# Attention followed by a feed-forward layer: one dealt list of matmuls per slot, and the copied form of the softmax rows from head 14 instead of head 18

## The chip, the cores and the metric

The kernel runs on one core of one Trainium2 chip. The metric is the device time of one execution in microseconds (us). The median of several runs is compared.

## The reference

Eight batches of eight heads; each head has 576 tokens of width 64. Every head is causal attention with a decay bias, and the result of all heads goes through a normalised feed-forward layer with a residual. Cut to what matters:

```python
scores = q @ k.T / sqrt(64)                      # 576 x 576 for each of 64 heads
cum    = cumsum(log(clip(f, 1e-4, 1)))
scores = where(causal, -1e9, scores + cum[:, None] - cum[None, :])
attn   = exp(scores - max); attn = attn / (sum + 1e-9)
x      = concat over heads of attn @ v           # 8 x 576 x 512
xn     = (x - mean) / sqrt(var + 1e-6) * g
out    = x + relu(xn @ w1) @ w2                  # 512 -> 2048 -> 512
```

All is float32. The kernel gets it from float32r matmuls of a high and a low part (two or three matmuls for one product).

## The kernel before, in words

The instructions of every engine stand in the order in which the Python code emits them; no scheduler moves them. TensorE runs its list in that order, and each matmul has a weight load (the stationary operand) of its own.

The outer loop runs over **slots** `u`: head `n` has four slots, t = 1 to 4, for its query blocks of 64 + 128, 128, 128 and 128 rows. A slot is named (n, t) below, and u = 4n + t - 1. In one slot the code emits pieces of several heads at once, in an order given by a string of letters (`ORDERS`; the entry with the largest first slot not above `u` holds):

- `Q`: `qk_mm`, the score matmuls `s` of this slot (L374 high part with 128 rows, L375 low part and bias with 66 rows; tiles `hi`, `xq`, `kl`). `S`, `e`, `B`: the softmax of the rows on VectorE (L398), ScalarE (L409) and GpSimd (L416).
- `D`: `move`. For heads from `MOVED` on, the finished softmax rows `p` are copied by a DMA of the sync queue into a float32r tile `pq`.
- `t`: `transpose_unit`, TensorE transposes of the rows into `tr` (for (n, 1) three, (n, 2) three, (n, 3) four, (n, 4) five instructions). From `pq` they are float32r (L440), from `p` float32 (L442). A 64-column block gives an output of 64 rows, so its weights are 64 columns wide; the other blocks are 128 wide. `h`, `l`: ScalarE and VectorE take `tr` out as high part `ph` and low part `pl` (L492, L497).
- `A`: `av_unit`, attn times v into `o` (L527), after t = 2 and t = 4; `F`, `a`: its result goes to `xs` (L561, L572) and by DMA to memory.
- `M`, `r`, `m`, `N`, `R`: the feed-forward, one step per slot. A chunk is 256 tokens and has 16 steps. `M` (`mm1`) makes twelve matmuls `h` of 256 columns (L604 to L606) from the chunk's four split inputs `x`; `N` (`mm2`) makes six of 512 columns (L626 to L628) into `acc` for the step before, and after a chunk's last step `chunk_out` (L685 on VectorE, `xt`). `R` loads the next chunk: `xr` by DMA (two buffers), split into `x` on ScalarE (L588) and VectorE (L589). If the four `x` are not yet split when `M` comes (`moe.can`), the slot has no `h`. A chunk is loaded only when its tokens are finished: `moe.limit` is worked out from the slot and the lag.

The transposes of a slot come `lag` slots later: `LAG` = 2 for heads whose rows stay in `p`, `LAG_MOVED` = 4 for those that are copied; `A` one slot later still. So with four slots of lag, slot (n+1, 1) holds `o` of head n - 1 (t = 4), `tr` of (n, 1) and `s` of (n+1, 0) and (n+1, 1).

The feed-forward starts at slot 35 (`FIRST_MOE`). Its steps that are left after the last slot run one behind the other in a tail. Ahead of that, weights are decoded (`WPrep`, first part of the kernel). PSUM has a ring of six banks for `s`, `tr`, `o`, `h`, `xp` and two more for `acc`.

What the change touches: `MOVED` (L33) and the first slot of the third entry of `ORDERS` (L56), `qk_mm`, `tr`, `transpose_unit`, `av_unit`, and in the slot loop `piece`. `moe.limit` depends on `MOVED`.

Of the kernel before, what the change touches and what calls it, by code (L numbers as in the profile page):

```python
# [9 lines left out]
F32R = mybir.dt.float32r  # L10
# [19 lines left out]
W2_WAIT = 2  # L30
ALL = 2 * NCHUNK * FT + W2_WAIT
LAG, LAG_MOVED = 2, 4
MOVED = 18  # L33
FIRST_MOE = 35
WARM = 36

# [16 lines left out]
ORDERS = [  # L53
    (0, "WwbQsSthAeMrgFmlLNPaRf"),
    (37, "WwbQSstAMhPelgLNFrfmBRa"),
    (70, "WwAthQFlMSPNgreamLRDB"),  # L56
]


# [1 line left out]
def attn_moe(ctx: ExitStack, tc: tile.TileContext, qk, v, f, g, w1, w2, out):  # L61
    nc = tc.nc
# [9 lines left out]
    mm = nc.tensor.matmul  # L72

    def bank(name):
        return ps.tile([P, 512], F32, tag="b", bufs=6, name=name)
# [5 lines left out]
    identr = const.tile([P, P], F32R, tag="identr", name="identr")  # L81
# [3 lines left out]
    ident = identr.bitcast(F32)  # L85
# [221 lines left out]
    def load(n):  # L307
        h = Head()
        h.n, h.plain, h.full = n, n < NPLAIN, n < NFULL
        h.normal, h.moved = {}, {}  # L310
        h.lag = LAG if n < MOVED else LAG_MOVED
        if h.plain:
# [49 lines left out]

    def qk_mm(h, t):
        q0, m, w = QT[t]
        cuts = [(0, w)] if w <= 512 else [(0, w // 2), (w // 2, w)]
        h.s = getattr(h, "s", {})
        h.s[t] = []
        for i, (a, z) in enumerate(cuts):
            sp = bank(f"s{h.n}_{t}_{i}")[:m, : z - a]
            xq, kl = h.xq[:, q0 : q0 + m], h.kl[:, a:z]  # L370
            if h.plain:
                mm(sp, xq, kl, start=True, stop=True)  # L372
            else:
                mm(sp, h.hi[:, 0, q0 : q0 + m], h.hi[:, 1, a:z], start=True, stop=False)  # L374
                mm(sp, xq, kl, start=False, stop=True)  # L375
            h.s[t].append((a, z, sp))

    corners = []

# [54 lines left out]
    def rows_of(h, t):  # L434
        return h.moved.get(t, h.p[t][0])

    def tr(out_, in_):
        m = in_.shape[0]
        if in_.dtype == F32R:
            nc.tensor.transpose(out_.bitcast(F32R), in_, identr[:m, :m])  # L440
        else:
            nc.tensor.transpose(out_, in_, ident[:m, :m])  # L442

# [2 lines left out]
    def transpose_unit(h, t):  # L448
        n = f"{h.n}"
        pt = rows_of(h, t)  # L450
        work_ = []
        if t <= 2:
            if t == 1:
                h.ph1 = work.tile([P, 704], F32 if h.full else F32R, tag="ph1", bufs=1, name=f"ph1_{n}")
                h.pl1 = None if h.full else late.tile([P, 384], F32R, tag="pl1", bufs=1, name=f"pl1_{n}")
            ph = h.ph1
            pl = ph if h.full else h.pl1
            tp = bank(f"tr{n}_{t}")
            if t == 1:
                tr(tp[0:64, 0:128], rows_of(h, 0)[:, 0:D])  # L460
                tr(tp[0:64, 64:192], pt[:, 0:64])
                tr(tp[:, 192:320], pt[:, 64:192])
                work_.append((tp[0:64, 0:192], ph[0:64, 0:192], ph[64:128, 0:192]))
                work_.append((tp[:, 192:320], ph[:, 320:448], pl[:, 0:128]))
            else:
                tr(tp[0:64, 0:128], pt[:, 0:64])
                tr(tp[:, 128:256], pt[:, 64:192])
                tr(tp[:, 256:384], pt[:, 192:320])
                work_.append((tp[0:64, 0:128], ph[0:64, 192:320], ph[64:128, 192:320]))
                work_.append((tp[:, 128:384], ph[:, 448:704], pl[:, 128:384]))  # L470
        else:
            if t == 3:
                h.ph2 = work.tile([P, 9 * P], F32 if h.full else F32R, tag="ph2", bufs=1, name=f"ph2_{n}")
                h.pl2 = None if h.full else late.tile([P, 7 * P], F32R, tag="pl2", bufs=1, name=f"pl2_{n}")
            c = 0 if t == 3 else P
            ph = h.ph2[:, : 8 * P].rearrange("p (k c) -> p k c", k=4)[:, :, c : c + P]
            pl = None if h.full else h.pl2[:, : 6 * P].rearrange("p (k c) -> p k c", k=3)[:, :, c : c + P]
            tp = bank(f"tr{n}_{t}").rearrange("p (k c) -> p k c", k=4)
            tr(tp[0:64, 0, :], pt[:, 0:64])
            for k in range(1, 4):  # L480
                tr(tp[:, k, :], pt[:, 64 + P * (k - 1) : 64 + P * k])
            work_.append((tp[0:64, 0, :], ph[0:64, 0, :], ph[64:128, 0, :]))
            work_.append((tp[:, 1:4, :], ph[:, 1:4, :], pl))
            if t == 4:
                tp = bank(f"tr{n}_4b")[:, :P]
                tr(tp, pt[:, 64 + 3 * P : 64 + 4 * P])
                work_.append((tp, h.ph2[:, 8 * P :], None if h.full else h.pl2[:, 6 * P :]))
        h.parts = work_

    def transposed_hi(h, t):  # L490
        for tp, hi, lo in h.parts:
            nc.scalar.copy(out=hi, in_=tp)  # L492
# [5 lines left out]

    def av_unit(h, t):
        po = bank(f"o{h.n}_{t}")  # L500

        if h.full:
            def fac(o, k, mv, first=False):
                st, mv = (h.vr[0:64, 0], mv[0:64]) if k == 0 else (h.vr[:, k], mv)
                mm(o, st, mv, start=first, stop=True, skip_group_check=True)  # L505

            if t == 2:
                ph = h.ph1
                fac(po[0:64, 0:320], 0, ph[:, 0:320], True)
                fac(po[0:64, 64:320], 1, ph[:, 320:576])  # L510
                fac(po[0:64, 192:320], 2, ph[:, 576:704])
                h.o = (po, S1, 0)
            else:
                ph = h.ph2
                for k in range(4):
                    fac(po[0:64, 0:256], k, ph[:, 256 * k : 256 * k + 256], k == 0)
                fac(po[0:64, 128:256], 4, ph[:, 8 * P :])
                h.o = (po, S - S1, S1)
            return

        vv = h.vv

        def both(k):
            return vv[:, k].rearrange("p a d -> p (a d)")

        def acc(o, st, mv, first=False):
            mm(o, st, mv, start=first, stop=True, skip_group_check=True)  # L527

        if t == 2:
            ph, pl, w, c0 = h.ph1, h.pl1, S1, 0  # L530
            acc(po[:, 0:320], both(0), ph[:, 0:320], True)
            acc(po[:, 64:320], both(1), ph[:, 320:576])
            acc(po[:, 192:320], both(2), ph[:, 576:704])
            acc(po[0:64, 64:320], vv[:, 1, 0, :], pl[:, 0:256])
            acc(po[0:64, 192:320], vv[:, 2, 0, :], pl[:, 256:384])
        else:
            ph, pl, w, c0 = h.ph2, h.pl2, S - S1, S1
            for k in range(4):
                acc(po[:, 0:256], both(k), ph[:, 256 * k : 256 * k + 256], k == 0)
            acc(po[:, 128:256], both(4), ph[:, 8 * P :])  # L540
            for k in range(1, 4):
                acc(po[0:64, 0:256], vv[:, k, 0, :], pl[:, 256 * (k - 1) : 256 * k])
            acc(po[0:64, 128:256], vv[:, 4, 0, :], pl[:, 6 * P :])
        h.o = (po, w, c0)

    xs_tile = {}

# [225 lines left out]
    hd = {}  # L773
# [12 lines left out]
    for u, slot in enumerate(slots):  # L786

        def before(k):
            return slots[u - k] if u >= k else None

        if slot is not None:
            n, t = slot
            h = hd[n]
        def turn(more):

            for lag in (LAG, LAG_MOVED):
                b = before(lag + more)
                if b is not None and hd[b[0]].lag == lag:
                    return b
            return None  # L800

        av, av_t = None, 0
        if turn(1) is not None and turn(1)[1] in (2, 4):
            av, av_t = hd[turn(1)[0]], turn(1)[1]
        moe.fetch_low(ALL if wp.done() else wp.ready())
        want = moe.can(wp.ready()) and u >= FIRST_MOE

        def piece(c):
            tu = turn(0)
            if c == "t" and tu is not None:  # L810
                transpose_unit(hd[tu[0]], tu[1])
            elif c == "h" and tu is not None:
                transposed_hi(hd[tu[0]], tu[1])
            elif c == "l" and tu is not None:
                transposed_lo(hd[tu[0]])
            elif c == "Q" and slot is not None:
                if t == 1:
                    qk_mm(h, 0)
                qk_mm(h, t)
            elif c == "A" and av is not None:  # L820
                av_unit(av, av_t)
            elif c == "S" and slot is not None:
                if t == 1:
                    softmax_a(h, 0)
# [15 lines left out]
            elif c == "R":  # L840
                moe.limit = min(NCHUNK, max(0, u - (LAG if u < 4 * MOVED else LAG_MOVED) - 1) // (4 * H) * S // C)
                moe.rest()
# [6 lines left out]
            elif c == "D":  # L849
                if before(1) is not None and hd[before(1)[0]].n >= MOVED:  # L850
                    move(hd[before(1)[0]], before(1)[1])
# [38 lines left out]
        for c in [o for first, o in ORDERS if first <= u][-1]:  # L890
            piece(c)
# [48 lines left out]
```

## Time and profile before

| what | value |
|---|---|
| median of 3 runs | 1207.02 us (1204.66 to 1209.07) |
| profiled execution, its own time | 1205.75 us |
| its span (first to last instruction) | 1204.0 us |
| TensorE matmuls | 8140, busy 98% of the span |
| VectorE, ScalarE, GpSimd busy | 63%, 53%, 35% |
| sync DMA queue | 60.7% of 16 engines |

The engines: PE is TensorE's matmuls, PEld its weight loads (they run beside matmuls), DVE is VectorE, ACT ScalarE, POOL GpSimd, SP the sync engine with its DMA queue. In the rows of a timeline the columns are start, length, engine, line, operation, names (out<-in), shapes and count; successive instructions of one form are merged, and the length is then that of the group. A length of a matmul is from its start until it has drained, so successive matmuls overlap: what one costs the next is the distance of the starts. For a matmul "128*64 128x128" means weights of 128 rows and 64 columns, and 128 moving columns.

### The profile page before, as it was taken

Reading aid. Unit: us, or ns where it says so; the run is one execution under the profiler, and the core shown is the slowest. Engines: PE = TensorE matmul, PEld = TensorE weight load, DVE = VectorE, ACT = ScalarE, POOL = GpSimd, SP = SyncE. Lnnn points to the kernel's source line nnn. Section 1 sums busy time; section 2 is a strip of 40 time slices with the busy share of each in tenths; the row PEclk is TensorE's granted clock in tenths of the full one; section 3 lists DMA queues with packets and bytes.
Section 4 is the critical chain, followed back from the end, with each engine's and each line's share of the span. In section 5 each row is a group of like instructions: output and inputs, shape, how many; then the busy total and the mean of one; then the engine's idle time right before and its main releaser. Section 6 shows DMA issues by size and latency. Waiting matters only on the chain.

```text
span 1204.0 us, 25987 instructions
## 1 busy us (share of the span) xinstructions
PE 1185.4 (98%) x8140; PEld 1057.7 (88%) x8140; DVE 756.5 (63%) x2884; ACT 643.2 (53%) x1920; POOL 426.1 (35%) x533
## 2 busy tenths in 40 slices
PE   7998999999999999999999999999999999999998
PEld 5666889999999999989999999999999999999997
DVE  5787647676768676766767676767676764233232
ACT  5888655565656565556565555556565642112111
POOL 3568544343434434344434433434444320000000
PEclk8999999999999999999999999999999999999999
DMA  7788653557666767567676666657666654434433
GB/s 204 228 239 272 204 163 118 154 172 214 219 202 202 234 187 231 170 217 218 212 224 199 209 207 205 221 181 231 199 220 213 189 182 135 128 121 126 139 108 94
DMA packets 171481, 228.50 MB, mean 190 GB/s; under 512 B 40784, under 2 KB 107856, under 8 KB 171344
## 3 DMA queue, kind: packets, MB, share of 16 engines
q1 hardware_dynamic: 171344, 226.85, 60.7%
q8 instruction: 65, 1.06, 0.4%
q14 instruction: 72, 0.59, 0.1%
HBM read 157.46 MB, written 23.36 MB: 150 GB/s over the span
## 4 chain that ended last, share of the span: by engine, by line
PE 92%; DVE 3%; ACT 2%; DMA 2%; issue 1%; SPq 0%; POOL 0%; DVEq 0%; ACTq 0%; POOLq 0%
PE h L604 11%; PE h L605 11%; PE h L606 11%; PE acc L626 11%; PE acc L627 11%; PE acc L628 11%; PE o L527 6%; PE s L374 4%; PE tr L440 4%; PE s L375 3%; PE o L505 3%; PE tr L442 2%; PE s L372 2%; PE xp L649 1%; PE pc L191 1%
## 5 line engine op out<-in xcount | busy, mean ns | idle before, releaser
L416 POOL TENSOR_SCALAR p<-p,st 64x64 f32<-64x64 f32 (+4 forms) x320 | 172.5, 543 | 489.4 <-DVE st L415 196.7
L604 PE MATMUL h<-x,w1h 128*128 128x256 f32 x1152 | 330.0, 286 | 0.8 <-ACT xs L558 0.8
L605 PE MATMUL h<-x,w1h 128*128 128x256 f32 x1152 | 325.6, 283 | 1.4 <-DVE st L414 1.3
L606 PE MATMUL h<-x,w1l 128*128 128x256 f32 x1152 | 325.3, 282 | 0.0
L612 ACT ACTIVATE hh<-h 128x256 fp32r<-128x256 f32 x288 | 110.3, 383 | 303.3 <-PE h L606 303.0
L617 DVE SCALAR_TENSOR_TENSOR hh<-h,hh 128x256 fp32r<-128x256 f32 x288 | 121.1, 421 | 172.9 <-ACT hh L612 170.9
L626 PE MATMUL acc<-w2h,hh 128*128 128x512 f32 x576 | 226.6, 393 | 0.0
L627 PE MATMUL acc<-w2s,hh 128*128 128x512 f32 x576 | 226.4, 393 | 0.0
L628 PE MATMUL acc<-w2h,hh 128*128 128x512 f32 x576 | 225.1, 391 | 0.0
L604 PEld LDWEIGHTS h<-x,w1h 128*128 128x128 f32 x1152 | 218.8, 190 | 6.2 <-ACT xs L558 1.0
L605 PEld LDWEIGHTS h<-x,w1h 128*128 128x128 f32 x1152 | 219.2, 190 | 5.2 <-DVE x L589 2.0
L606 PEld LDWEIGHTS h<-x,w1l 128*128 128x128 f32 x1152 | 219.2, 190 | 0.0
L409 ACT ACTIVATE p<-p,st 64x64 f32<-64x64 f32 (+4 forms) x320 | 178.3, 558 | 49.2 <-DVE st L398 45.6
L492 ACT CAST ph<-tr 64x128 fp32r<-64x128 f32 (+4 forms) x416 | 117.8, 332 | 130.9 <-PE tr L440 76.5
L398 DVE CUSTOM_DVE_ANT_0 p<-s,mask 64x64 f32<-64x64 f32 (+4 forms) x320 | 130.7, 420 | 17.0 <-DMA pq<-p 5.2
L497 DVE TENSOR_TENSOR ph<-tr,ph 64x192 fp32r<-64x192 f32 x208 | 62.6, 301 | 108.7 <-ACT ph L492 83.6
L628 PEld LDWEIGHTS acc<-w2h,hh 128*128 128x128 f32 x576 | 108.2, 188 | 24.1
L626 PEld LDWEIGHTS acc<-w2h,hh 128*128 128x128 f32 x576 | 109.4, 190 | 12.6
L627 PEld LDWEIGHTS acc<-w2s,hh 128*128 128x128 f32 x576 | 109.3, 190 | 11.8
L374 PE MATMUL s<-hi 128*64 128x64 f32 x336 | 105.4, 336 | 1.3 <-POOL hi L352 1.0
L497 DVE TENSOR_TENSOR pl<-tr,ph 128x128 fp32r<-128x128 f32 x208 | 95.3, 458 | 4.6
L375 PE MATMUL s<-kl,xq 66*64 66x64 f32 x336 | 98.0, 296 | 0.0
(86 smaller groups left out, 1784.5 us busy)
## 6 DMA issues: line engine op xcount, KB each, us to landing
w2s<-w2d SPq DMA_DIRECT2D x288, 256.0 KB
raw<-in_qk_dram SPq DMA_DIRECT2D x56, 576.0 KB
wr<-in_w_dram SPq DMA_DIRECT2D x32, 512.0 KB
pq<-p SPq DMA_DIRECT2D x46, 288.0 KB
pq<-p SPq DMA_DIRECT2D x46, 224.0 KB
vr<-in_v_dram SPq DMA_DIRECT2D x64, 160.0 KB
out_dram<-xt SPq DMA_DIRECT2D x36, 256.0 KB
xq<-hi SPq DMA_DIRECT2D x56, 144.0 KB
```

The lines of the kernel that those rows point to most:

```text
L374: mm(sp, h.hi[:, 0, q0 : q0 + m], h.hi[:, 1, a:z], start=True, stop=False)
L375: mm(sp, xq, kl, start=False, stop=True)
L398: nc.vector.tensor_tensor_reduce(out=pt[:m, a:z], in0=sp, in1=mask[:m, off + a : off + z], scale=-SCALE, scalar=3.0e38 if i == 0 else st[: ...
L409: nc.scalar.activation(pt[:m, :w], pt[:m, :w], AF.Exp, bias=st[:m, i : i + 1], scale=-1.0, accum_out=st[:m, 2:3])
L416: nc.gpsimd.tensor_scalar(out=pt[:m, :w], in0=pt[:m, :w], scalar1=st[:m, 3:4], scalar2=1.0, op0=ALU.mult, op1=ALU.mult)
L497: nc.vector.tensor_tensor(out=lo, in0=tp, in1=hi.bitcast(F32), op=ALU.subtract)
L604: mm(ph, w1h[:, k, fs], c.x[k][:, 0, :], start=(k == 0), stop=False)
L605: mm(ph, w1h[:, k, fs], c.x[k][:, 1, :], start=False, stop=False)
L606: mm(ph, w1l[:, k, fs], c.x[k][:, 0, :], start=False, stop=(k == KT - 1))
L626: mm(c.acc[i], h[:, 0, ts_], w2h[:, j, :], start=(j == 0), stop=False)
L627: mm(c.acc[i], h[:, 0, ts_], low, start=False, stop=False)
L628: mm(c.acc[i], h[:, 1, ts_], w2h[:, j, :], start=False, stop=(j == FT - 1))
```

## The change

Two things. First, `MOVED` goes from 18 to 14 and the third order string starts at slot 56 instead of 70: heads 14 to 17 are copied and transposed in float32r, with four slots of lag. Second, the functions that made matmuls now return a list of them. For heads with a lag of four slots the piece `A` makes all three lists (`a` for attn times v, `b` for the transposes, `q` for the scores) and emits them in the order that `dealt` gives; in other heads the lists are emitted as before.

```diff
-MOVED = 18
+MOVED = 14
...
-    (70, "WwAthQFlMSPNgreamLRDB"),
+    (56, "WwAthQFlMSPNgreamLRDB"),
...
+    def dealt(t, u1, a, b, q):
+        if t == 4 and q:
+            return a[:5] + a[8:] + b[:2] + q[:1] + a[5:6] + b[2:] + q[1:2] + a[6:7] + q[2:3] + a[7:8] + q[3:]
+        if t == 4:
+            return a[:5] + a[8:] + b[:2] + a[5:6] + b[2:] + a[6:8]
+        if t == 2:
+            return a[:3] + a[4:] + b + a[3:4] + q
+        return (a + b if u1 else b[1:] + b[:1]) + q
...
+            if c in "AtQ" and tu is not None and hd[tu[0]].lag == LAG_MOVED:
+                if c == "A":
+                    a = av_unit(av, av_t) if av is not None else []
+                    b = transpose_unit(hd[tu[0]], tu[1])
+                    q = []
+                    if slot is not None:
+                        q = (qk_mm(h, 0) if t == 1 else []) + qk_mm(h, t)
+                    run(dealt(av_t, tu[1] == 1, a, b, q))
+            elif c == "t" and tu is not None:
+                run(transpose_unit(hd[tu[0]], tu[1]))
...
+                run((qk_mm(h, 0) if t == 1 else []) + qk_mm(h, t))
...
+                run(av_unit(av, av_t))
```

`a` for t = 4 has nine matmuls: four of 256 and one of 128 columns with weights 128 wide, then three of 256 and one of 128 with weights 64 wide.

**TensorE, slot (38, 1) before and now.** In the order of instructions `o36_4` is `a`, `tr37_1` is `b`, `s38_0` and `s38_1` are `q`; the last two numbers are the width of the weights and the moving columns. Before:

```order
L527 MATMUL o36_4_8690<-ph2_36_8572,vv36_8480 128x128
L527 MATMUL o36_4_8690<-pl2_36_8573,vv36_8480 64x256 x3
L527 MATMUL o36_4_8690<-pl2_36_8573,vv36_8480 64x128
L440 MATMUL tr37_1_8702<-identr_74,pq37_0_8557 64x128
L440 MATMUL tr37_1_8702<-identr_74,pq37_1_8559 64x128
L440 MATMUL tr37_1_8702<-identr_74,pq37_1_8559 128x128
L374 MATMUL s38_0_0_8708<-hi38_8474 64x64
L375 MATMUL s38_0_0_8708<-kl38_8475,xq8_1143 64x64
L374 MATMUL s38_1_0_8711<-hi38_8474 128x192
L375 MATMUL s38_1_0_8711<-kl38_8475,xq8_1143 128x192
```

The same slot of the change:

```order
L513 MATMUL o36_4_8730<-ph2_36_8607,vv36_8520 128x128
L513 MATMUL o36_4_8730<-pl2_36_8608,vv36_8520 64x128
L456 MATMUL tr37_1_8733<-identr_74,pq37_0_8597 64x128
L456 MATMUL tr37_1_8733<-identr_74,pq37_1_8599 64x128
L368 MATMUL s38_0_0_8734<-hi38_8514 64x64
L513 MATMUL o36_4_8730<-pl2_36_8608,vv36_8520 64x256
L456 MATMUL tr37_1_8733<-identr_74,pq37_1_8599 128x128
L368 MATMUL s38_0_0_8734<-kl38_8515,xq8_1143 64x64
L513 MATMUL o36_4_8730<-pl2_36_8608,vv36_8520 64x256
L368 MATMUL s38_1_0_8735<-hi38_8514 128x192
L513 MATMUL o36_4_8730<-pl2_36_8608,vv36_8520 64x256
L368 MATMUL s38_1_0_8735<-kl38_8515,xq8_1143 128x192
```

The three matmuls of 256 columns with narrow weights now stand between short matmuls and wide weights.

**TensorE, from slot (17, 3) to the first step of chunk 2.** `acc1` is the last `mm2` of chunk 1, `h2_0` the first `mm1` of chunk 2. Before:

```order
L628 MATMUL acc1_1_2612<-w2h_126,hh1_15_3490 128x512
L442 MATMUL tr17_2_3561<-identr_74,p17_2_3450 64x128
L442 MATMUL tr17_2_3561<-identr_74,p17_2_3450 128x128 x2
L374 MATMUL s17_4_0_3567<-hi17_3135 128x288
L375 MATMUL s17_4_0_3567<-kl17_3136,xq9_1286 128x288
L374 MATMUL s17_4_1_3570<-hi17_3135 128x288
L375 MATMUL s17_4_1_3570<-kl17_3136,xq9_1286 128x288
L604 MATMUL h2_0_3575<-x2_0_3435,w1h_124 128x256
```

The change, from the scores of the same slot (17, 4):

```order
L368 MATMUL s17_4_1_3554<-kl17_3125,xq9_1286 128x288
L513 MATMUL o16_4_3586<-ph2_16_3493,vv16_3402 128x256 x4
L513 MATMUL o16_4_3586<-ph2_16_3493,vv16_3402 128x128
L513 MATMUL o16_4_3586<-pl2_16_3494,vv16_3402 64x128
L456 MATMUL tr17_1_3589<-identr_74,pq17_0_3483 64x128
L456 MATMUL tr17_1_3589<-identr_74,pq17_1_3485 64x128
L368 MATMUL s18_0_0_3590<-hi18_3396 64x64
L513 MATMUL o16_4_3586<-pl2_16_3494,vv16_3402 64x256
L456 MATMUL tr17_1_3589<-identr_74,pq17_1_3485 128x128
```

Chunk 2 started in slot (17, 4); now slot (17, 4) has neither `h` nor `acc`, and `h2_0` comes behind `s18_1`. In the same way all later chunks up to chunk 5 start one slot later.

**VectorE, at the start of chunk 4.** `xt3` is `chunk_out` of chunk 3, `x4_2` and `x4_3` are splits for chunk 4, whose first step `h4_0` was in slot (26, 1) and is in slot (26, 2) now. Before, from the end of the softmax of (25, 4):

```order
L398 ISA st25_4_5595 128x1
L685 SCALAR_TENSOR_TENSOR xt3_0_5213<-acc3_0_4658,rs3_5216,xt3_0_5213 128x512
L685 SCALAR_TENSOR_TENSOR xt3_1_5344<-acc3_1_4659,rs3_5216,xt3_1_5344 128x512
L589 TENSOR_TENSOR x4_2_5609<-xr4_2_5562,x4_2_5609 128x256
L589 TENSOR_TENSOR x4_3_5612<-xr4_3_5565,x4_3_5612 128x256
L414 TENSOR_SCALAR st25_4_5595<-st25_4_5595 128x1
```

The change, one slot later:

```order
L404 ISA st26_1_5679 128x1
L358 CAST vv25_5687<-vr25_5479 128x5x64
L709 SCALAR_TENSOR_TENSOR xt3_0_5290<-acc3_0_4727,rs3_5293,xt3_0_5290 128x512
L709 SCALAR_TENSOR_TENSOR xt3_1_5435<-acc3_1_4728,rs3_5293,xt3_1_5435 128x512
L596 TENSOR_TENSOR xs24_320_5671<-o24_4_5647,ot24_320_5672 64x256
L613 TENSOR_TENSOR x4_3_5703<-xr4_3_5637,x4_3_5703 128x256
```

`x4_3` now waits behind `vv25`, `xt3` and `xs24`. In the kernel before, the same row of work (`vv33`, two `xt5`, `xs32`, `x6_3`) stands at the start of chunk 6, in slot (34, 1); there the change has the `xt5` behind `x6_3`, and slot (34, 1) has its `h`.

More of the change, by code (lines that the diff above doesn't have):

```diff
@@ L364, in qk_mm, with mm @@
         q0, m, w = QT[t]
+        todo = []
+        def mm(*a, **k):
+            todo.append(lambda: nc.tensor.matmul(*a, **k))
         cuts = [(0, w)] if w <= 512 else [(0, w // 2), (w // 2, w)]
@@ L376, in qk_mm @@
             h.s[t].append((a, z, sp))
+        return todo
     corners = []
@@ L435, in rows_of @@
         return h.moved.get(t, h.p[t][0])
[L437 to L442, printed above, removed]
     def transpose_unit(h, t):
@@ L450, in transpose_unit, with tr @@
         pt = rows_of(h, t)
-        work_ = []
+        work_, todo = [], []
+        def tr(out_, in_):
+            m = in_.shape[0]
+            if in_.dtype == F32R:
+                todo.append(lambda: nc.tensor.transpose(out_.bitcast(F32R), in_, identr[:m, :m]))
+            else:
+                todo.append(lambda: nc.tensor.transpose(out_, in_, ident[:m, :m]))
         if t <= 2:
@@ L488, in transpose_unit @@
         h.parts = work_
+        return todo
     def transposed_hi(h, t):
@@ L500, in av_unit, with mm @@
         po = bank(f"o{h.n}_{t}")
+        todo = []
+        def mm(*a, **k):
+            todo.append(lambda: nc.tensor.matmul(*a, **k))
         if h.full:
@@ L518, in av_unit @@
                 h.o = (po, S - S1, S1)
-            return
+            return todo
         vv = h.vv
@@ L544, in av_unit @@
         h.o = (po, w, c0)
+        return todo
+    def dealt(t, u1, a, b, q):
[6 more added lines that the diff above has]
+        return (a + b if u1 else b[1:] + b[:1]) + q
     xs_tile = {}
@@ L806, in attn_moe, with run @@
         want = moe.can(wp.ready()) and u >= FIRST_MOE
+        def run(todo):
+            for emit in todo:
+                emit()
         def piece(c):
             tu = turn(0)
-            if c == "t" and tu is not None:
-                transpose_unit(hd[tu[0]], tu[1])
+            if c in "AtQ" and tu is not None and hd[tu[0]].lag == LAG_MOVED:
[8 more added lines that the diff above has]
+                run(transpose_unit(hd[tu[0]], tu[1]))
             elif c == "h" and tu is not None:
@@ L816, in piece @@
             elif c == "Q" and slot is not None:
-                if t == 1:
-                    qk_mm(h, 0)
-                qk_mm(h, t)
+                run((qk_mm(h, 0) if t == 1 else []) + qk_mm(h, t))
             elif c == "A" and av is not None:
-                av_unit(av, av_t)
+                run(av_unit(av, av_t))
             elif c == "S" and slot is not None:
```

## The prediction

> **What bounds the kernel now.** I read the page first: engines, the slices, the chain.
>
> ```profile
> span 1204.0 us, 25987 instructions
> PE 1185.4 (98%) x8140; PEld 1057.7 (88%) x8140; DVE 756.5 (63%) x2884; ACT 643.2 (53%) x1920; POOL 426.1 (35%) x533
> PEclk8999999999999999999999999999999999999999
> PE 92%; DVE 3%; ACT 2%; DMA 2%; issue 1%; SPq 0%; POOL 0%; DVEq 0%; ACTq 0%; POOLq 0%
> ```
>
> TensorE is the bound, at full clock nearly everywhere. So a gain must come from shorter TensorE work, and "busy" does not say whether a step is stream or weight load. For that I took the timeline of matmuls, and of weight loads, in slot (46, 1), whose list is the first one shown with the change.
>
> ```profile
> 701.51 0.70 PE L527 MATMUL o<-ph,vv 128*128 128x256 f32 x5
> 702.05 0.58 PE L527 MATMUL o<-pl,vv 128*64 128x256 f32 x4
> ```
>
> The next two are two steps of `h` in slot (46, 2).
>
> ```profile
> 706.46 0.28 PE L604 MATMUL h<-x,w1h 128*128 128x256 f32 x1
> 706.58 0.28 PE L605 MATMUL h<-x,w1h 128*128 128x256 f32 x1
> ```
>
> The starts of two matmuls of 256 columns are 0.12 us apart. The first group is four of 256 and one of 128: 0.54 - 0.48 = 0.06 for 128 columns. So a stream costs some 0.03, 0.06, 0.09, 0.12 for 64, 128, 192, 256 columns (the first and third are estimates in proportion).
>
> ```profile
> 702.62 0.13 PEld L374 LDWEIGHTS s<-hi 128*64 128x64 f32 x1
> 702.68 0.14 PEld L375 LDWEIGHTS s<-kl,xq 66*64 66x64 f32 x1
> 702.74 0.19 PEld L374 LDWEIGHTS s<-hi 128*128 128x128 f32 x1
> 702.85 0.19 PEld L375 LDWEIGHTS s<-kl,xq 66*128 66x128 f32 x1
> 702.96 0.19 PEld L604 LDWEIGHTS h<-x,w1h 128*128 128x128 f32 x1
> ```
>
> The other slot shows loads for wide transposes:
>
> ```profile
> 705.88 0.23 PEld L440 LDWEIGHTS tr<-identr,pq 128*128 128x128 f32 x2
> 706.05 0.19 PEld L374 LDWEIGHTS s<-hi 128*128 128x128 f32 x1
> ```
>
> In the first of these fences the loads set the pace: 0.055 to 0.06 apart where they are 64 wide, 0.11 where 128 wide, though the streams beside them are only 0.03 to 0.09. Loads for float32r transposes, 128 wide, are 0.17 / 2 = 0.085 apart. The rule that I take from this: a step lasts as long as the longer of its own stream and the load of the next matmul. Long matmuls (256, 512 columns) hide every load; short ones ahead of wide weights do not.
>
> By the Trainium skill (TensorE: Matmul & The Clock Gate, section LDWEIGHTS) a load takes columns / 1.2 ns, 53 and 107 ns, whatever the rows. The ordinary loads agree, 66 rows included; the transposes' 85 do not. With 107 for them the dealing would give 0.07 us more a head, 3.3 in all; I go by 85.
>
> **The change, part by part.** *Dealing, by slots of a head.* Only the part of a load that sticks out counts. For (n, 1), before: narrow transpose to wide 0.025, `s` 64 to 64 0.025, 64 to 192 0.08, 192 to 192 0.02, 192 to `h` 0.02; sum 0.17. Now: two narrow scores ahead of a narrow `o` 0.025 each, the last one ahead of `h` 0.02; sum 0.07. Saved 0.10. For (n, 3): three steps into wide transposes 0.025 each and one into the scores 0.05; now a 256-column matmul stands ahead of the scores; saved 0.05. For (n, 2) and (n, 4): the narrow transpose goes last, so the first wide load lies under a 512-column matmul; saved 0.025 each. Together 0.20 a head (0.21 with prices to the ns), for 50 heads 10.6 us. Six of the new neighbours of a head (a score ahead of `o`, a wide transpose ahead of a score and the like) stand in no row; such a step can cost from its stream alone to 0.05 more, the excess of a load of 0.11 over a stream of 0.06. I take the rule's value, since the narrow rows 702.62 to 702.74 are the nearest, and give the range 0.01 for each, 3 us in all.
>
> *Float32r in heads 14 to 17.* Fifteen transposes a head change form.
>
> ```profile
> 249.74 0.60 PE L442 MATMUL tr<-identr,p 128*64 128x128 f32 x4
> 250.18 0.27 PE L442 MATMUL tr_4b<-identr,p 128*128 128x128 f32 x1
> 250.21 0.36 PE L604 MATMUL h<-x,w1h 128*128 128x256 f32 x1
> 250.41 0.28 PE L605 MATMUL h<-x,w1h 128*128 128x256 f32 x1
> ```
>
> From the first transpose to the second `h` it is 0.67; less 0.12 for the first `h`, 0.55 for five, 0.11 each, 1.64 a head. In copied form, in the old order, by the rule: 0.06 + 0.085 + 0.06 in (n, 1); 2 x 0.085, 3 x 0.085 and 4 x 0.085, each with 0.11 for the load of the scores, in the others; 1.30. Saved 0.35, for four heads 1.4. Sum with the dealing 12.0; all instructions of both orders priced one by one give 12.1, which I take.
>
> *Copies.* Twenty more DMAs on the sync queue. One issue:
>
> ```profile
> 703.77 0.47 SPq L431 DMA_DIRECT2D pq<-p  x1
> ```
>
> That is 20 x 0.47 = 9 us of queue time in 16 slots, over some 62 us; behind them stand `w2s`, `xr` and `raw`, all fetched a slot or more ahead. I price them at nothing, with up to 1 us of waiting if that cover is gone. GpSimd does the same work.
>
> *Later ends.* In (n, 1) the last matmul of `o` ends 0.37 later (1.31 instead of 0.94 after 701.51, so 702.8), and the first scores start 0.5 earlier, in a bank that `tr_4b` held.
>
> ```profile
> 699.86 0.28 DVE L497 TENSOR_TENSOR pl<-tr_4b,ph 128x128 fp32r<-128x128 f32 x1
> 703.41 0.37 ACT L561 COPY ot<-o 64x256 f32<-64x256 f32 x1
> ```
>
> ScalarE takes `o` only at 703.41, and the bank was free by 700.14; both are covered by more than 0.5 us. Price nothing; without that cover it would be up to 0.4 us in two slots of each head, 40 us, which I count with the slower side.
>
> *Chunk starts.* The slots without `h` move. What they cost now, with a like slot beneath each:
>
> ```profile
> 241.52:245.35 3.83, 3.83 (x29) 3.51 (x29) 2.72 (x9) 1.52 (x4) 0.43 (x1) 1.00 0.15 44
> 256.46:260.50 4.04, 3.60 (x30) 3.22 (x29) 3.80 (x12) 1.89 (x6) 1.83 (x3) 1.00 0.82 274
> 384.81:387.72 2.91, 2.52 (x22) 2.12 (x19) 2.83 (x11) 2.86 (x9) 0.68 (x1) 1.00 0.83 294
> 400.07:403.39 3.32, 3.32 (x27) 2.99 (x25) 2.55 (x12) 2.66 (x9) 1.36 (x2) 1.00 0.60 205
> 512.72:528.44 15.72, 13.99 (x87) 11.96 (x86) 10.56 (x40) 7.70 (x24) 6.23 (x8) 0.89 0.75 231
> 531.77:544.08 12.31, 12.31 (x93) 11.44 (x92) 7.04 (x26) 6.16 (x18) 4.97 (x7) 1.00 0.67 214
> ...
> 700.59 0.39 PE L628 MATMUL acc<-w2h,hh 128*128 128x512 f32 x1
> 700.82 0.39 PE L626 MATMUL acc<-w2h,hh 128*128 128x512 f32 x1
> ```
>
> (Columns: stretch, length, busy time and count of PE, PEld, DVE, ACT, POOL, clock, DMA share, GB/s.) Six `mm2` matmuls are 6 x 0.23 = 1.38, missing in the first slot of a late chunk. Slot (26, 1) lost 2.91 - (3.32 - 1.38) = 1.0; slots (34, 2) to (34, 4) lost 15.72 - (12.31 - 1.38) = 4.8; slot (17, 4), against (16, 4) less `mm2`, with five `o` more (0.50) and four float32 transposes for three (0.11),, lost 4.04 - 3.06 = 1.0. Sum 6.8. My prices give 12.26 for the undisturbed three slots, so the rule holds to half a per cent.
>
> ```profile
> 251.72 0.40 PE L626 MATMUL acc<-w2h,hh 128*128 128x512 f32 x1
> 253.54 0.42 DVE L617 SCALAR_TENSOR_TENSOR hh<-h,hh 128x256 fp32r<-128x256 f32 x1
> 258.26 0.41 DVE L589 TENSOR_TENSOR x<-xr,x 128x256 fp32r<-128x256 f32 x1
> ...
> 513.91 1.39 DVE L685 SCALAR_TENSOR_TENSOR xt<-acc,rs,xt 128x512 f32<-128x512 f32 x2
> 514.57 0.39 PE L604 MATMUL h<-x,w1h 128*128 128x256 f32 x1
> 515.56 0.41 DVE L589 TENSOR_TENSOR x<-xr,x 128x256 fp32r<-128x256 f32 x1
> 516.02 0.38 PE L605 MATMUL h<-x,w1h 128*128 128x256 f32 x1 [1.06 <-DVE st L414]
> ```
>
> At chunk 6 TensorE stood from 514.57 to 516.02 for the last split `x`, which VectorE did behind `xt`; after it the granted clock fell (0.89 in that stretch). After the change: chunk 6 has its `h` in (34, 1) and `x` ahead of `xt`, so 0 (0 to 1). Chunk 4 gets VectorE's order of the old chunk 6, so 4.8 (1 to 5, the low end being what it loses today). Chunk 2 has two slots without `h`: from `hh` of the last step to the last `x` VectorE took 258.26 - 253.54 = 4.7; now the list between has also the `tr16_4` parts, two more splits and the softmax of (17, 4), less `vv`, some 2.7 more. From the end of that `h` TensorE has two `mm2` (2.8), three `o` and `tr` groups with their scores (3.6) and nine `h` (1.2), 7.6 us, until it needs the last `x`; `hh` starts 1.8 after that end (251.72 to 253.54), so VectorE is ready at 1.8 + 7.4 + 0.4 = 9.6; a wait of 2, with the clock after it 3.5 (1.3 to 6). Sum 8.3 against 6.8: 1.5 lost.
>
> *Sum.* 12.1 - 1.5 = 10.6. The profiled execution took 1205.75, of it 1204.0 span and 1.75 around it: 1195.2. The median of the runs is 1.27 above it, 1207.02: **1196.4 us**.
>
> **The rivals.**
>
> *Switching widths empties the array (slower).* Changes between weights 64 and 128 wide go from 10 to 14 a head, 200 in all. Price, from the row
>
> ```profile
> L605 PE MATMUL h<-x,w1h 128*128 128x256 f32 x1152 | 325.6, 283 | 1.4 <-DVE st L414 1.3
> ```
>
> 0.283 - 0.12 = 0.16 of fill and drain that is now hidden: 32 us, so 1228. It turns the result from 10.6 / 200 = 0.053 us a switch. Against it: in the first fence the group ends with a wide matmul of 128 columns ahead of a narrow one and that step took 0.06, its stream. The Trainium skill (TensorEngine Tiling (Array Packing), section Key Properties) says that changing the tiling mode drains TensorE; the switches of this trace show no such drain. Chance 0.04.
>
> *Heavy chunk starts.* All three at their upper ends, 12 instead of 8.3: 1200.1, with a move's wait of 1, 1201. For it: the DMA share of 0.75 to 0.83 there; against: VectorE's list is lighter at chunk 6. Chance 0.13. *Light chunk starts*, 2.3 in all: 1190.4. Chance 0.12.
>
> *The dealing does nothing*, if the 0.11 belongs to the score matmuls and not to what stands ahead of their loads: only 1.4 - 1.5, so 1207. Against it: `s` to `h` costs the same 0.11, and a load beside 512 columns none. Chance 0.05.
>
> **How the numbers follow.** The forecast keeps 0.66; its own range is 1193 to 1200 (stalls 2.5 either way, 1 to 3 for the prices). With heavy and half of the light starts, and runs that lay 2 us about their median, 1191 to 1202. A measurement tells 0.3%, 3.6 us, from no change. Faster: forecast, heavy, light, 0.91; within: dealing does nothing, 0.05; slower: the drain, with the lost cover of the later ends, 0.04.
>
> **What the new profile would show.** Weight loads 0.11 apart gone between the scores of (n, 1); a quiet head some 0.21 us shorter; heads 14 to 17 without L442-like float32 transposes; waits for `x` near (18, 1) and (26, 2), none near (34, 2). I am wrong if the quiet heads keep their length, if TensorE waits for `pq` or `o` in each slot, or if the clock falls at more than two chunk starts.

## The result and the profile after

The changed kernel took 1198.99 us in the median (1198.44 to 1199.87, 4 runs), the kernel before 1207.29 on the same chip (1204.66 to 1209.07, 4 runs). The ratio is 0.9934, 95% interval 0.9914 to 0.9953: 8.3 us faster, 6 to 10 by the interval. Forecast were 10.6 us and 1196.4.

The page of the changed kernel: span, busy times, clock by slices, shares of the chain of waits.

```profile
span 1198.1 us, 26129 instructions
PE 1178.0 (98%) x8140; PEld 1051.9 (88%) x8140; DVE 756.9 (63%) x2884; ACT 644.2 (54%) x1920; POOL 427.1 (36%) x533
PEclk8998999999999999999999999999999999999999
PE 93%; DMA 2%; DVE 2%; ACT 2%; issue 1%; POOL 0%; SPq 0%; DVEq 0%; ACTq 0%; POOLq 0%
```

TensorE is still the bound, with as many instructions; 7.4 us of its busy time and 5.8 of the weight loads' are gone. The two profiled spans differ by 5.9 us. Slot (13, 1), ahead of the first changed slot, already starts 1.0 us later in this profile (181.43 against 180.39 us). That is not the change. The 8 in the fourth slice of PEclk is a stretch from 106.0 to 112.8 us, ahead of the first changed slot, in which the granted clock was 0.50; the kernel before has none there. Of the profiles that are alike up to slot (13, 1), those with this stretch have the slot at 181.4 to 182.1 (the changed kernel, e1, e7), those without it at 179.3 to 180.5 (before, e2, e3). Behind the slot the gain is 6.9.

The next two fences are from the timelines of matmuls, before and after. Each holds the first `o` of a slot (n, 1) and the same of the next head. Between them lies one quiet head, one without the extra matmuls of a chunk's end.

```profile
638.19 0.70 PE L527 MATMUL o<-ph,vv 128*128 128x256 f32 x5
653.83 0.70 PE L527 MATMUL o<-ph,vv 128*128 128x256 f32 x5
```

```profile
510.17 0.70 PE L513 MATMUL o<-ph,vv 128*128 128x256 f32 x5
525.67 0.70 PE L513 MATMUL o<-ph,vv 128*128 128x256 f32 x5
```

15.64 us before, 15.50 now: 0.14 saved a head, where 0.21 was forecast. This is the main miss, and it repeats: from head 36 to head 63 the two profiles part by 3.8 us, 0.14 a head.

To see where it is lost I split every slot into its list (from the first matmul of the list to the first `h`) and the rest (twelve `h`, six `acc`). Medians over the quiet slots behind 560 us, in us:

| slot | list before | list after | rest before | rest after | saved | priced |
|---|---|---|---|---|---|---|
| (n, 1) | 1.535 | 1.441 | 2.834 | 2.835 | 0.093 | 0.107 |
| (n, 2) | 0.580 | 0.547 | 2.817 | 2.818 | 0.033 | 0.028 |
| (n, 3) | 1.272 | 1.243 | 2.804 | 2.846 | -0.013 | 0.053 |
| (n, 4) | 0.991 | 0.954 | 2.807 | 2.817 | 0.027 | 0.028 |

Three slots came out as priced, to 0.014 us. Slot (n, 3) gained nothing.

The weight loads of slot (n, 1) in the new kernel, behind those of the five wide `o`:

```profile
604.46 0.17 PEld L456 LDWEIGHTS tr<-identr,pq 128*64 128x64 f32 x2
604.57 0.13 PEld L368 LDWEIGHTS s<-hi 128*64 128x64 f32 x1
604.63 0.14 PEld L513 LDWEIGHTS o<-pl,vv 128*64 128x64 f32 x1
604.71 0.14 PEld L456 LDWEIGHTS tr<-identr,pq 128*128 128x128 f32 x1
604.80 0.14 PEld L368 LDWEIGHTS s<-kl,xq 66*64 66x64 f32 x1
604.87 0.14 PEld L513 LDWEIGHTS o<-pl,vv 128*64 128x64 f32 x1
604.93 0.19 PEld L368 LDWEIGHTS s<-hi 128*128 128x128 f32 x1
```

The run of loads 0.11 apart between short scores is gone: wide loads now alternate with narrow ones, under a narrow `o` of 256 columns, at spacings of 0.06 to 0.09.

The slot that gained nothing. First from the timeline of before, a slot (n, 3): the four transposes in one row, the two scores, the first `h`, then the first `acc` and the first row of the next list.

```profile
583.14 0.45 PE L440 MATMUL tr<-identr,pq 128*64 128x128 f32 x4
583.43 0.44 PE L374 MATMUL s<-hi 128*128 128x448 f32 x1
583.70 0.37 PE L375 MATMUL s<-kl,xq 66*128 66x448 f32 x1
583.91 0.28 PE L604 MATMUL h<-x,w1h 128*128 128x256 f32 x1
...
585.34 0.40 PE L626 MATMUL acc<-w2h,hh 128*128 128x512 f32 x1
...
586.72 0.29 PE L440 MATMUL tr<-identr,pq 128*64 128x128 f32 x2
```

The same of the new kernel, in slot (30, 3), and then the `acc` of slot (31, 3), one head later:

```profile
455.50 0.47 PE L456 MATMUL tr<-identr,pq 128*64 128x128 f32 x4
455.81 0.30 PE L513 MATMUL o<-pl,vv 128*64 128x256 f32 x1
455.95 0.37 PE L368 MATMUL s<-hi 128*128 128x448 f32 x1
456.15 0.37 PE L368 MATMUL s<-kl,xq 66*128 66x448 f32 x1
...
457.80 0.40 PE L650 MATMUL acc<-w2h,hh 128*128 128x512 f32 x1
...
459.18 0.28 PE L456 MATMUL tr<-identr,pq 128*128 128x128 f32 x2
...
473.26 0.40 PE L650 MATMUL acc<-w2h,hh 128*128 128x512 f32 x1
...
474.67 0.38 PE L456 MATMUL tr<-identr,pq 128*128 128x128 f32 x3
```

Two things show. In the list, from the first transpose to the second score it took 0.56 before (583.14 to 583.70) and 0.65 now, with one more matmul of 256 columns (0.12) in it: 0.03 saved, where the step counted 0.05. And the six `acc`, which nothing in the change touches, take 1.38 us at 455 but 1.41 at 473, by the same instructions in the same order and at full clock. From head 31 on slot (n, 3) is in that slower rhythm in all heads but one; heads 20 and 22 to 24 had it too, heads 27 to 30 did not. The kernel before already had it in one head of four: where the list of (n, 3) begins with four transposes for a chunk's end (`xp`), its six `acc` take 1.40 us. More on it below.

Chunk 2. The fences show stretches of the new kernel (columns as in the prediction; each runs from the first scores with 128-wide weights of one slot to those of the next, so it holds the next slot's `o` and `tr`), then matmuls with the waits in front of them, then VectorE.

```profile
254.29:258.80 4.51, 2.25 (x20) 1.87 (x19) 4.27 (x14) 2.16 (x7) 0.67 (x2) 1.00 0.77 242
258.80:262.21 3.41, 2.62 (x20) 2.10 (x19) 2.05 (x11) 3.00 (x9) 0.67 (x1) 1.00 0.85 236
```

```profile
257.31 0.78 PE L513 MATMUL o<-ph,vv 128*128 128x256 f32 x5 [2.25 <-DVE ph L506]
...
260.38 0.38 PE L628 MATMUL h<-x,w1h 128*128 128x256 f32 x1 [0.39 <-ACT x L612]
...
254.21 1.41 DVE L709 SCALAR_TENSOR_TENSOR xt<-acc,rs,xt 128x512 f32<-128x512 f32 x2
255.53 0.47 DVE L596 TENSOR_TENSOR xs<-o,ot 64x320 f32<-64x320 f32 x1
255.93 0.74 DVE L613 TENSOR_TENSOR x<-xr,x 128x256 fp32r<-128x256 f32 x2
...
256.97 0.28 DVE L506 TENSOR_TENSOR ph<-tr,ph 64x128 fp32r<-64x128 f32 x1
```

By the prediction's prices the two slots last 2.86 and 1.42 us too long, 4.3 in all (3.5 forecast). The long wait is not for `x`: TensorE stood 2.25 us for `ph`, which VectorE reached only behind `xt`, `xs` and two splits. The wait for `x` came later and was short.

Chunk 4, the same views:

```profile
386.07:390.96 4.89, 3.47 (x27) 2.82 (x25) 4.76 (x19) 3.03 (x11) 2.78 (x5) 1.00 0.84 205
390.96:396.51 5.55, 3.80 (x27) 3.18 (x26) 1.60 (x6) 1.81 (x6) 2.61 (x3) 1.00 0.86 304
```

```profile
389.13 0.38 PE L629 MATMUL h<-x,w1h 128*128 128x256 f32 x1 [0.99 <-DVE st L420]
...
396.08 0.45 PE L456 MATMUL tr<-identr,pq 128*128 128x128 f32 x3 [1.75 <-DMA pq<-p]
```

Losses of 2.34, 1.90 and 0.49 in (26, 2) to (26, 4), 4.7 together (4.8 forecast). The first holds the wait of 0.99 for the last split `x` (VectorE's split at 388.66 ended at 389.07) and one of 0.41 for `ph` behind it. The second is the copy `pq`, which the forecast priced at nothing. Chunk 6 has no wait: its slot (34, 2) starts and goes through at the pace of a quiet one.

### The profile page after: what moved, and what is told of

Its sections match the earlier page's. It is cut to its first block, busy times and chain, and to the rows that moved or that the text cites. A ratio compares the mean times of both kernels' runs of the same rounds, so it can differ in the third digit from the quotient of the medians.

```text
span 1198.1 us, 26129 instructions
## 1 busy us (share of the span) xinstructions
PE 1178.0 (98%) x8140; PEld 1051.9 (88%) x8140; DVE 756.9 (63%) x2884; ACT 644.2 (54%) x1920; POOL 427.1 (36%) x533
## 3 DMA queue, kind: packets, MB, share of 16 engines
q8 instruction: 65, 1.06, 0.4%
## 4 chain that ended last, share of the span: by engine, by line
PE 93%; DMA 2%; DVE 2%; ACT 2%; issue 1%; POOL 0%; SPq 0%; DVEq 0%; ACTq 0%; POOLq 0%
PE h L628 12%; PE h L629 11%; PE h L630 11%; PE acc L650 11%; PE acc L651 11%; PE acc L652 11%; PE o L513 9%; PE s L368 9%; PE tr L456 4%; PE tr L458 1%; DMA wr<-in_w_dram 1%; PE xp L673 1%; PE pc L191 1%; DMA pq<-p 1%; ACT p L415 1%
## 5 line engine op out<-in xcount | busy, mean ns | idle before, releaser
L368 PE MATMUL s<-hi 128*64 128x64 f32 x336 | 102.3, 312 | 1.3 <-POOL hi L352 1.0
```

Of the source, the lines that this page charges most:

```text
L368: todo.append(lambda: nc.tensor.matmul(*a, **k))
```

## The experiments

No kernel below leaves out any work. In batch 1 (e1 to e4) the kernel before took 1205.32 us on that chip (17 runs), in batch 2 (e5 to e7) 1205.24 (13 runs).

**e1: only `MOVED` and the order string.** The kernel before with two numbers changed:

```diff
-MOVED = 18
+MOVED = 14
-    (70, "WwAthQFlMSPNgreamLRDB"),
+    (56, "WwAthQFlMSPNgreamLRDB"),
```

> The kernel before with only the copied form from head 14 (MOVED 14, third order from slot 56), matmuls in the old order. Theory (prices of weight loads and streams, chunk starts by VectorE's order): TensorE saves 1.8 us, the chunk starts are those of the change and cost 9.0 instead of 6.8, so 0.4 slower than before, 1207.7; chunk 2 loses 4.3 around slot (18, 1), chunk 4 loses 4.7 around (26, 2), chunk 6 nothing. Rival (the copied form brings the larger part of the measured 8.3): 1201 to 1203.

1206.2 us (12 runs), ratio 1.0003 [0.9992, 1.0015]. The float32r gain of four heads is eaten by the chunk starts: its profile loses 2.57 + 1.76 at chunk 2, 2.13 + 2.41 + 0.38 at chunk 4 and nothing at chunk 6, 9.2 in all, against 6.8 before. So this half of the change is worth nothing that these runs can tell.

**e2: only the dealing.** The changed kernel with `MOVED` back at 18 and the string at slot 70.

> The change with MOVED 18 and the third order from slot 70 again, so the dealing alone, in 46 heads. Theory: quiet heads 0.14 shorter as in the changed kernel's trace, 46 x 0.14 = 6.4, chunk starts as before (1.0, 1.0, 4.8): 1200.9. Rival 1 (the price of the prediction, 0.21 a head, holds where the chunk starts are the old ones): 9.5 us, 1197.8. Rival 2 (the dealing gives little): above 1205.

1198.96 us (6 runs), ratio 0.9945 [0.9931, 0.9960]: 6.4 us less than before, for 46 heads 0.14 a head. The prediction's 0.21 would have given 9.7. So the gain lies in the dealing, and it has the size of the 0.14 a head that the trace shows.

**e3: slot (n, 3) in the old order.**

```diff
         if t == 2:
-            return a[:3] + a[4:] + b + a[3:4] + q
+            return a + b + q
```

> The change, but in slots with o of t = 2 the old order (a, b, q). Theory: there the dealing gained nothing, since the twelve h and six acc behind it run 0.04 slower; undone, slot (n, 3) takes 4.076 instead of 4.089, h and acc 2.804, a quiet head 15.487 instead of 15.500: 0.6 us faster than the change, 1198.4. Rival 1 (the price of the prediction, 0.0525 a slot): 2.6 us slower, 1201.6. Rival 2 (the slower h and acc have another cause than the order ahead of them): slot 4.118, 1.4 slower, 1200.4.

1200.25 us (6 runs), ratio 0.9956 [0.9940, 0.9973]; not faster. Slot (n, 3) is quick again behind its list (2.818), and its list longer (1.278 against 1.243): dealing it does save 0.03. But now slot (n, 4), which was not touched, has the slow rhythm in three heads of four (median 2.847 against 2.817). So the rhythm does not belong to the dealt order of (n, 3), and my theory, that taking that order out gains 0.6, fell.

**e4: the next chunk loaded and split two at a time**, aimed at the chunk starts:

```diff
-            for i in range(4 if left == 0 else 1):
+            for i in range(4 if left == 0 else 2 if left < 2 else 1):
...
-            for i in range(2 if left < 2 else 1):
+            for i in range(2 if left < 4 else 1):
```

> The change, but the next chunk is loaded and split two pieces at a time when fewer than four (load) or two (split) steps are left, so chunk 4 has its four x one slot earlier and no slot without h. Theory: the 4.7 us at chunk 4 come from the last split x behind chunk_out on VectorE, and go to 0 to 1; chunk 2 stays at 4.3: about 1195. Rival (VectorE or the DMA is the bound around a chunk start, so the same time is lost a slot or two later): 1199, no change.

1194.82 us (5 runs), ratio 0.9912 [0.9897, 0.9928], as the theory had it. By the ratios that is some 3 us below the changed kernel, with intervals that overlap, so the trace has to show where it comes from. The stretch of chunk 4's start, from its windows:

```profile
384.00:400.00 16.00, 16.00 (x118) 14.72 (x118) 11.78 (x45) 10.04 (x33) 6.85 (x9) 1.00 0.86 278
```

TensorE is busy through all 16 us; both the wait for `x` and the one for `pq` are gone. Chunk 2 still loses 2.81 + 1.64. So chunk 4's 4.7 us hang on how early the four inputs are loaded and split, and the wait for `pq` goes with it. In the queue the last loads `xr` are issued at 382.0 and the two copies `pq` at 391.0, in the changed kernel at 385.4 and 391.9; that the copies landed late because the work crowded behind one late start is argued from this, not shown.

**e5: e4, and from slot 56 (head 14) on chunks released one slot earlier:**

```diff
-... max(0, u - (LAG if u < 4 * MOVED else LAG_MOVED) - 1) ...
+... max(0, u - (LAG if u < 4 * MOVED else LAG_MOVED) - (u < 4 * MOVED)) ...
```

> The kernel with the chunk loaded and split two pieces at a time, and from slot 56 on the limit on chunks one slot earlier, so that chunk 2 has one slot without h instead of two. Theory: what chunk 2 loses goes from 4.3 to 1 to 2.5, chunk 4 stays at 0 to 1: 2 to 3.3 us less than the kernel with the loads alone, ratio to before 0.989. Rival (VectorE's work between the last hh of chunk 1 and the last x of chunk 2 is the bound, not the empty slots): ratio 0.991 as with the loads alone.

1192.92 us (4 runs), ratio 0.9898 [0.9881, 0.9916], the fastest of all kernels with e6. The interval overlaps e4's, so the trace decides: chunk 2 loses 1.9 instead of 4.5, and 1.2 come back in the stretch from the scores of (33, 4) to those of (34, 1). What TensorE waits for there:

```profile
257.13 0.38 PE L629 MATMUL h<-x,w1h 128*128 128x256 f32 x1 [0.52 <-DVE x L613]
...
511.15 0.24 PE L368 MATMUL s<-kl,xq 66*64 66x64 f32 x1 [0.85 <-DMA xq<-hi]
```

The wait of 2.25 for `ph` is gone; a new short one for a DMA, `xq`, has come in its place at chunk 6.

**e6: e5, with the narrow transpose last in slot (n, 3) too.**

```diff
-            return a[:3] + a[4:] + b + a[3:4] + q
+            return a[:3] + a[4:] + b[1:] + b[:1] + a[3:4] + q
```

> As the kernel with two pieces at a time and the earlier limit, but in slots with o of t = 2 the narrow transpose stands last of its four, ahead of the narrow o. By the rule of loads and streams (n, 3) is as long as dealt, 1.243 up to the first h. Theory A (h and acc run slower in one slot of a head by how the list ahead of them ends): the end of the list is the same, so h and acc stay at 2.846 there and the time is the same. Theory B (it hangs on the exact time at which the first h starts): the slower 2.846 goes to another slot of the head or vanishes; vanished, a head is 0.03 to 0.04 shorter, 1.5 to 2 us in all.

1193.18 us (4 runs), ratio 0.9897 [0.9882, 0.9912]: no difference from e5 that these runs can tell. Slot (n, 3) is now at 4.056, with the quick rest (2.818), and the slow rhythm has gone to (n, 4) (2.848), though the list of (n, 3) ends as in the changed kernel: theory A fell. A quiet head takes 15.48, 0.02 less than in e5, some 1 us in all; the chunk starts lose 1.2 more than e5's (among them a wait of 1.28 for `x` in chunk 6), and that hides it.

**e7: more changes of width.** The changed kernel with the narrow `o` of (n, 1) put between the wide ones, and its transposes and scores in the old order:

```diff
-            return a[:5] + a[8:] + b[:2] + q[:1] + a[5:6] + ...
+            return a[:1] + a[5:6] + a[1:2] + a[6:7] + a[2:3] + a[7:8] + a[3:5] + a[8:] + b + q
```

> The change, but in slots with o of t = 4 and scores the three narrow matmuls of 256 columns stand one by one between the wide ones of 256 columns, and transposes and scores follow in the old order. It takes the cover from the short matmuls of that slot and adds six changes of weight width where every load is covered by 256 columns. Theory (a change of width costs nothing): the slot takes what it took before the change up to the first h, 1.535. Rival (a change of width drains the array, 0.05 to 0.16 each): 1.8 to 2.5.

1202.5 us (8 runs), ratio 0.9979 [0.9969, 0.9990]. The list's beginning in its timeline, weights of 128 and 64 columns in turn:

```profile
637.35 0.28 PE L513 MATMUL o<-ph,vv 128*128 128x256 f32 x1
637.47 0.28 PE L513 MATMUL o<-pl,vv 128*64 128x256 f32 x1
637.59 0.28 PE L513 MATMUL o<-ph,vv 128*128 128x256 f32 x1
637.71 0.28 PE L513 MATMUL o<-pl,vv 128*64 128x256 f32 x1
```

Each step is 0.12, the stream of 256 columns, as between matmuls of one width. The list has ten changes of width, that of before four, and takes 1.523 against 1.535. It is also the counter-test of the dealing: with the long narrow `o` no longer between the short matmuls and the wide weights, the list has lost nearly all that it had gained (1.441). Slot (n, 3), with the same instructions as in the changed kernel, is quick here (2.811 against 2.846), though only the list two slots ahead of it differs; one head of four has the slow rhythm in (n, 4).

## Why the prediction was right, and where it was not

**The bound, and what dealing gains: right.** Steps lasting the longer of stream and next load gave what slots (n, 1), (n, 2) and (n, 4) save, to 0.014 us. e2 puts the gain on the dealing, and e7, which takes the long matmuls away from the short ones, gives the gain of (n, 1) back.

**The term that was mis-sized: (n, 3), "saved 0.05".** It measured 0.013 lost. Two parts are measured. The list gained 0.03, not 0.05: before, the four transposes and the first score cost some 0.01 less than priced, and now the narrow `o` takes 0.136 up to the score behind it, where 0.118 was priced. And the rest of the slot became 0.042 longer, which no price of a single step contains. With (n, 1) 0.014 short, a quiet head saves 0.14, not 0.21; over 46 to 50 heads that is some 3.3 of the 10.6 us.

What makes the slow rhythm is not settled. The runs show that it isn't a property of an instruction pair: it sits mostly in (n, 4) in e3 and e6, in (n, 3) in e5 and the changed kernel, in e7 in (n, 4) of one head of four, before in (n, 3) of one head of four, and in the changed kernel it settles in (n, 3) at head 31 with the order unchanged. It costs 0.03 us in one slot of four (2.846 against 2.818; the rest of the 0.042 stands in the quick slots of the later kernels too), about 1 us of the whole.

**Heads 14 to 17: right in sum.** e1 came out even, as 1.4 to 1.8 gained by the prices and 2.4 lost in the trace would have it, within its interval (-1.0 to 1.8 us).

**Chunk starts: right in sum, wrong in what waits for what.** 9.0 us lost in all against 8.3 forecast, 6.8 before. At chunk 2 (3.5 forecast, 4.3 measured) I let TensorE wait for the last `x` alone. The same VectorE list delays `ph`, and `o` needs that first; asking only for the last item of the late queue missed the one that is needed earliest. And in this profile the fall of the clock that was to follow did not come; in e1, e3, e4 and e7, with a like wait for `ph` (2.25 to 2.33 us), it did (0.50 for 3.41 us), and the wait for `x` was gone, so that chunk 2 lost much the same (4.3 in e1, 4.5 in e4). At chunk 4 the total of 4.8 was taken from the old chunk 6, and it fitted to 0.1 by another path: that is luck. In rows of windows, before at chunk 6 and after at chunk 4:

```profile
518.00:520.00 2.00, 2.00 (x10) 1.92 (x10) 1.16 (x4) 1.27 (x5) 1.51 (x3) 0.50 0.97 377
```

```profile
392.00:394.00 2.00, 2.00 (x15) 1.74 (x13) 0.84 (x2) 0.79 (x2) 1.92 (x2) 1.00 1.06 407
394.00:396.00 2.00, 0.33 (x2) 0.00 (x0) 0.00 (x0) 0.00 (x0) 0.03 (x1) 1.00 0.79 246
```

Before, the clock was at 0.50 and TensorE busy throughout. Now it ran at 1.00, finished early and stood for `pq`, while the DMA engines moved about as much (377 and 407 GB/s). The losses are equal, 1.88 and 1.90. In e1 and e7 the clock halved at chunk 4 (2.41 and 1.51 lost, of it 0.76 and nothing in waiting for `pq`), in e3 it did not (1.44 of waiting, 1.70 lost). So at full clock it was the copy that set the end there, and a halved clock took the place of part or all of that wait. The Trainium skill (TensorE: Matmul & The Clock Gate, section What's actually happening) says that the window which decides the clock runs freely. The clock records of the nine traces agree: in each, all changes of the granted clock lie whole multiples of 3.41 us apart, at places that differ against the kernel's start. At chunk 2 this tells like waits apart, by two such windows of e4 and two of the changed kernel:

```profile
255.33:258.75 3.42, 1.89 (x17) 1.75 (x18) 3.07 (x12) 0.77 (x4) 0.65 (x1) 1.00 0.83 277
258.75:262.16 3.41, 3.41 (x17) 3.03 (x16) 2.17 (x11) 3.05 (x10) 0.75 (x1) 0.50 0.81 239
```

```profile
252.78:256.20 3.42, 2.27 (x15) 1.76 (x13) 3.29 (x8) 2.36 (x8) 1.45 (x2) 1.00 0.70 208
256.20:259.61 3.41, 2.30 (x21) 2.16 (x22) 2.64 (x11) 0.76 (x3) 0.64 (x1) 1.00 0.74 232
```

Both waits took 2.25 us. In e4 most of it fell into one window, TensorE was busy for 55% of that, and the next ran at 0.50; in the changed kernel a border cut the wait, each of the two was busy for two thirds, and the clock stayed. Between 250 and 600 us every halved window of the nine traces followed one that was busy for 33 to 62%; among the windows that were not followed by a halved one, a single one was as low (49%, at the wait for `pq` in the changed kernel), so busy time by itself is not the whole rule.

**The copies: nothing, with "up to 1 us of waiting" if the cover goes.** The cover went at one place, 1.75 us; e4, in which that wait is gone, ties it to the late chunk start.

**The rivals.** The drain at changes of width is out: e7 has six more in each (n, 1) and its list is 0.012 shorter than that of before. The Trainium skill (TensorEngine Tiling (Array Packing), section Key Properties) has a change of tiling mode drain TensorE; changes between weights 64 and 128 columns wide cost nothing here beyond the stream (0.12 a step in e7). "The dealing does nothing" is out by e2. Of the heavy chunk starts a fifth came, 9.0 on the way from 8.3 to 12; the light ones did not come.

**The sum.** 10.6 - 3.3 - 0.7 = 6.6, against 6.9 between the two profiles behind slot (13, 1), and 8.3 by the medians, whose interval holds both.

## What to carry to other kernels

Where TensorE is full, list for each matmul its own stream and the load of the next one: putting a long matmul ahead of wide weights paid the difference, and changing between 64 and 128 columns cost nothing. Check such a sum on one repeated stage: here it lost a third, more than half of that to an effect that no pair of instructions shows. When a queue comes late, look for the item on it that is needed earliest, not only for the last, and split a late batch of inputs earlier: here that was worth some 3 us, and some 4 with the earlier release (e4 and e5 beside the changed kernel, each by its ratio to the kernel before; the intervals are 2 us wide to either side), where the dealing gave 6.4.

## What the runs showed of the hardware that was not expected

The same six matmuls of 512 columns take 1.38 or 1.41 us at the same granted clock, and keep one of the two rhythms for many heads; which slot is slow can change with a list two slots ahead. What sets it is open. Waits of 1.06 and 0.41 us close together were followed by a halved clock before (0.50 in the row above), waits of 0.99 and 0.41 at the like place by none. The clock changed only on a grid of 3.41 us, whose place against the kernel differed from profile to profile, so the same wait can cost a halved window or not.
